# First halves of two experts filled from the scan's first three chunks, a reordered chunk, and rows kept by chunk

## Chip, core and metric

The program runs on one core of a Trainium2 chip. The metric is device time in microseconds (us) of one execution, the median of several. Five engines work beside each other, each through its own queue in order: TensorE (PE; its weight loads are shown apart as PEld), VectorE (DVE), ScalarE (ACT), GpSimd (POOL) and SyncE (SP). DMAs are issued from the queues of SP, ACT and POOL. An instruction that waits holds up everything behind it on its own engine.

## The reference

Two blocks follow each other. The first is a chunked state-space scan over 4 batches, 8 heads and 768 steps; the second sends each of the 3072 rows that come out (256 wide) to one of 8 experts, chosen by cosine similarity, and weighs the expert's output.

```python
# scan, per batch and head, chunk after chunk
cum = np.cumsum(la); L = np.exp(cum[:, None] - cum[None, :]) * causal
y[chunk] = ((C @ B.T) * L) @ x + (C @ state) * np.exp(cum)[:, None]
state = np.exp(sum(la)) * state + sum over j of exp(cum[-1] - cum[j]) * outer(B[j], x[j])
# rows: y laid out as (batch * step, head * dim), x below
logits = (x / norm(x)) @ (emb / norm(emb)).T / tau
e = argmax(logits); gate = softmax(logits)[e]
out = gate * (relu(x @ w1[e]) @ w2[e])          # w1: 256 x 1024, w2: 1024 x 256, float32
```

## The kernel before

**Scan.** `mamba` walks over six chunks of 128 steps (`NC` = 6), all four batches together. In chunk c TensorE spreads the decays of the next chunk, takes the inner products C B in two halves (`inner(k, c, 0)` and `inner(k, c, 1)`, into the four banks of `pg`), and VectorE masks each half (`mask_inner`, L336, 1536 elements wide). Between the two halves stands `finish(c-1)` (L395), which turns the previous chunk's outputs into rows and computes their logits; `keep_rows` copies the rows out of PSUM on ScalarE and `send_rows` stores them to `y_rows` in DRAM through SP. Then come the contributions of the states, the outputs of the two halves, `first_outputs`, and the state sums of the next chunk. GpSimd scales x of the next chunk (`scale_x`, `scale_first_half`) and makes U from T (`decay_states`); `add_sums` needs U at the next chunk's start.

**Routing beside the scan.** For each chunk, `pick` (VectorE) finds each token's expert and GpSimd adds the counts before every block of tokens into `pre`. `rank_rows` (two small matmuls) gives each token its rank in its expert, `places` (ten VectorE operations) turns ranks into a place: one of `NT` = 4 tiles of `TR` = 104 rows an expert, so 416 places. `locate` (eight matmul instructions, L580) writes the token's number to its place; the table `idx` is summed over chunks. At the end of each chunk stand, in this order: `pick(c-1)`, `decay_states(c+1)`, `places(c-2)`, `rank_rows(c-1)`, `locate(c-2)`. After the last chunk the remaining steps follow one after the other, and `end_places` makes the gather indices `gi` and the target rows `to`.

**Mixture.** A `Job` is one expert: four indirect gathers on GpSimd (L738) fetch its 416 rows; `turn_x` transposes them on TensorE; `gates` computes the weights, with squares and an exponential on ScalarE, a square root as a power on GpSimd (L759) and small VectorE steps; `up(f)` makes one of eight hidden blocks (L784; each float32 matmul shows as two instructions, so four a block), its result is copied through a ReLU by ScalarE and VectorE in turn; `down` makes the outputs (L798), `out` transposes them back (L812), multiplies by the gate (L814) and scatters the rows (L815). `moe` overlaps a job's `out` with the next job's `up`. Expert weights have three buffers. `leftover` is a loop for experts with more than 416 rows; where no expert has more, its blocks do not run.

The scan, up to `end_places`, is in an order written by hand (`manual_schedule`). The mixture is ordered by a scheduler, which also puts some of its instructions early: the weight loads of experts 1 and 2 were issued on SP between 42 and 69 us, ahead of later stores of rows.

Of the kernel before, what the change touches and what calls it, by code (L numbers as in the profile page):

```python
# [17 lines left out]
Q = 128  # L18
# [8 lines left out]
LEFT = (T - CAP) // Q + E  # L27
LG, Y1, W = 128, 128 + E, DM + E
# [379 lines left out]
def send_rows(k, c):  # L408
    k.nc.sync.dma_start(
        k.y_d.rearrange("(b c p) w -> c p b w", b=NB, p=Q)[c], k.ld[c].rows[:]  # L410
    )
# [50 lines left out]
def route_consts(k):  # L462
# [10 lines left out]
    k.tok1 = ints("tok1", [128, NC, NB], [[Q, NC], [S, NB]], 1, 1)  # L473
# [18 lines left out]
    k.idx = k.const.tile([TR, E * NT], F32, name="idx")  # L492
    k.at, k.eq, k.hot = {}, {}, {}
# [82 lines left out]
def locate(k, c):  # L576

    eq, hot = k.eq.pop(c), k.hot.pop(c)
    for b in range(NB):
        k.nc.tensor.matmul(  # L580
            k.pz[:TR, 1, 424 : 424 + E * NT], lhsT=hot[:, b, :],
            rhs=eq[:].rearrange("p (b e) t -> p b (e t)", b=NB)[:, b], start=(b == 0), stop=(b == NB - 1),
        )


def keep_located(k, c):
    if c == 0:
        k.nc.scalar.copy(out=k.idx[:], in_=k.pz[:TR, 1, 424 : 424 + E * NT])
        return
    i = k.work.tile([TR, E * NT], F32, name="ix", tag="ix")  # L590
    k.nc.scalar.copy(out=i[:], in_=k.pz[:TR, 1, 424 : 424 + E * NT])
    k.nc.gpsimd.tensor_tensor(out=k.idx[:], in0=k.idx[:], in1=i[:], op=ALU.add)


def end_places(k):
    nc = k.nc
    c = NC - 1
    locate(k, c)
    n = k.pz[:, 1, 456 : 456 + E]
    nc.tensor.matmul(n, lhsT=k.ones[:], rhs=k.pre[:, NU, :], start=True, stop=True)  # L600
    nc.vector.tensor_tensor(out=k.idx[:], in0=k.idx[:], in1=k.pz[:TR, 1, 424 : 424 + E * NT], op=ALU.add)
# [7 lines left out]
    nc.vector.scalar_tensor_tensor(  # L609
        out=k.to[:], in0=k.idx[:], scalar=-1.0, in1=none[:], op0=ALU.add, op1=ALU.add  # L610
    )
# [4 lines left out]
def mamba(k):  # L616
# [29 lines left out]
    for c in range(NC):  # L646
# [3 lines left out]
        if c in (3, 4):  # L650
            load_weights(k, 0, (c - 3,))
        if c + 1 < NC:
            spread_decays(k, c + 1)
# [3 lines left out]
        mask_inner(k, c, 0)  # L657
        if c + 1 < NC:
            scale_c(k, c + 1)
# [14 lines left out]
        if c + 1 < NC:  # L674
            split_b(k, c + 1)
            mask_c(k, c + 1)
            scale_x(k, c + 1, nc.gpsimd)
            scale_first_half(k, c + 1, nc.gpsimd)
            if c in (0, 3):
                between(k, c + 1, 4 if c == 0 else NC)  # L680
            pass_c(k, c + 1)
        if c == 0:
            decays(k, 1)
            block_ends(k, 1)
            inverses(k, 1)
# [3 lines left out]
        outputs(k, c, 1)  # L689
        first_outputs(k, c)  # L690
# [3 lines left out]
        if c == 1:  # L694
            turn_inverses(k, 1, k.pz[:, 0, 0:256])
        if c > 0:
            pick(k, c - 1)
        if c + 1 < NC:
            decay_states(k, c + 1)
        if c >= 2:  # L700
            places(k, c - 2)
        if c > 0:
            rank_rows(k, c - 1)
            keep_ranks(k, c - 1)
        if c >= 2:
            locate(k, c - 2)
            keep_located(k, c - 2)
    c = NC - 1
    finish(k, c)
    keep_rows(k, c)  # L710
    send_rows(k, c)
    places(k, c - 1)
    pick(k, c)
    locate(k, c - 1)
    keep_located(k, c - 1)
    rank_rows(k, c)
    keep_ranks(k, c)
    places(k, c)
    end_places(k)
    k.step = k.ints("step", [128, LEFT], [[1, LEFT]], 0, 0)  # L720
    k.part = k.ints("part", [128, 1], [[0, 1]], 0, 1)


class Job:


    def __init__(s, k, nt, tr, w1, w2):
        s.k, s.nt, s.tr, s.w1, s.w2 = k, nt, tr, w1, w2

    def load(s, e):  # L730
        k = s.k
        s.x = k.p.tile([s.tr, s.nt, KD * Y1], F32, name="xg", tag="xg")
        for i in range(s.nt):
            s.gather(i, k.gi[:, NT * e + i : NT * e + i + 1])
        s.to = k.to[:, NT * e : NT * e + NT]

    def gather(s, i, at):
        s.k.nc.gpsimd.indirect_dma_start(  # L738
            out=s.x[:, i, 0:W], out_offset=None, in_=s.k.y_d[:, :],
            in_offset=bass.IndirectOffsetOnAxis(ap=at, axis=0), bounds_check=T - 1, oob_is_err=False,  # L740
        )

    def gates(s):

        k, nc, tr, nt = s.k, s.k.nc, s.tr, s.nt
        m = k.p.tile([tr, nt], F32, name="gm", tag="gm")
        nc.vector.reduce_max(out=m[:], in_=s.x[:, :, LG : LG + E], axis=AX.X)  # L747
        l = k.p.tile([tr, nt, E], F32, name="gl", tag="gl")
        nc.vector.tensor_tensor(
            out=l[:], in0=s.x[:, :, LG : LG + E], in1=m[:].unsqueeze(2).to_broadcast([tr, nt, E]), op=ALU.subtract  # L750
        )
        r = k.p.tile([tr, nt], F32, name="gr", tag="gr")
        for i in range(nt):
            sq = k.p.tile([tr, KD, 128], F32, name="sq", tag="sq")
            nc.scalar.activation(  # L755
                sq[:], s.x[:, i, :].rearrange("p (j w) -> p j w", j=KD)[:, :, 0:128], ACT.Square,
                accum_out=r[:, i : i + 1],
            )
        nc.gpsimd.tensor_tensor(out=r[:], in0=r[:], in1=k.half[0:tr, 0:nt], op=ALU.pow)  # L759
        nc.vector.tensor_scalar_add(r[:], r[:], 1e-6)  # L760
        nc.vector.reciprocal(out=r[:], in_=r[:])
        nc.vector.tensor_tensor(out=l[:], in0=l[:], in1=r[:].unsqueeze(2).to_broadcast([tr, nt, E]), op=ALU.mult)
        nc.scalar.activation(l[:], l[:], ACT.Exp)
        s.gate = k.p.tile([tr, nt], F32, name="gate", tag="gate")
        nc.vector.reduce_sum(out=s.gate[:], in_=l[:], axis=AX.X)
        nc.vector.tensor_scalar_add(s.gate[:], s.gate[:], 1e-9)
        nc.vector.reciprocal(out=s.gate[:], in_=s.gate[:])

    def turn_x(s):
        k, nc, tr, nt = s.k, s.k.nc, s.tr, s.nt  # L770
        s.xT = k.p.tile([128, KD, nt * tr], F32, name="xT", tag="xT")
        for j in range(KD):
            t = k.ps.tile([128, nt, tr], F32, name="xt", tag="xt", bufs=2)
            for i in range(nt):
                nc.tensor.transpose(t[:, i, :], s.x[:, i, Y1 * j : Y1 * j + 128], k.ident[:tr, :tr])  # L775
            nc.vector.tensor_copy(out=s.xT[:, j, :], in_=t[:].rearrange("p t r -> p (t r)"))

    def up(s, f):
        k, nc = s.k, s.k.nc
        if f == 0:  # L780
            s.hT = k.p.tile([128, KF, s.nt * s.tr], F32, name="hT", tag="hT")
        t = k.ps.tile([128, s.nt * s.tr], F32, name="hp", tag="hp", bufs=3)
        for j in range(KD):
            nc.tensor.matmul(  # L784
                t[:], lhsT=s.w1[:, j, 128 * f : 128 * f + 128], rhs=s.xT[:, j, :], start=(j == 0), stop=(j == KD - 1)
            )
        if f % 2 == 0:
            nc.scalar.activation(s.hT[:, f, :], t[:], ACT.Relu)  # L788
        else:
            nc.vector.tensor_scalar_max(s.hT[:, f, :], t[:], 0.0)  # L790

    def down(s):
        k, nc = s.k, s.k.nc
        s.yT = k.p.tile([128, KD, s.nt * s.tr], F32, name="yoT", tag="yoT")
        for j in range(KD):
            t = k.ps.tile([128, s.nt * s.tr], F32, name="yp", tag="yp", bufs=2)
            for f in range(KF):
                nc.tensor.matmul(  # L798
                    t[:], lhsT=s.w2[:, f, 128 * j : 128 * j + 128], rhs=s.hT[:, f, :],
                    start=(f == 0), stop=(f == KF - 1),  # L800
                )
            if j % 2 == 0:
                nc.scalar.copy(out=s.yT[:, j, :], in_=t[:])
            else:
                nc.vector.tensor_copy(out=s.yT[:, j, :], in_=t[:])  # L805

    def out(s):
        k, nc, tr = s.k, s.k.nc, s.tr
        for i in range(s.nt):
            t = k.ps.tile([128, DM], F32, name="ot", tag="ot", bufs=1)  # L810
            for j in range(KD):
                nc.tensor.transpose(t[:tr, 128 * j : 128 * j + 128], s.yT[:, j, tr * i : tr * i + tr], k.ident[:])  # L812
            y = k.p.tile([tr, DM], F32, name="yo", tag="yo", bufs=4)
            nc.vector.tensor_scalar_mul(y[:], t[:tr, :], s.gate[:, i : i + 1])  # L814
# [9 lines left out]
def moe(k):  # L824
    jobs = {}

    def begin(e):
        jobs[e] = j = Job(k, NT, TR, k.w1t[e], k.w2t[e])
        j.load(e)

    def ready(e):
        jobs[e].turn_x()
        jobs[e].gates()

    begin(0)
    load_weights(k, 1)
    ready(0)
    load_weights(k, 2)
    begin(1)
    for e in range(E + 1):  # L840
        for f in range(KF):
            if e < E:
                jobs[e].up(f)
            if f == 1 and e > 0:
                jobs.pop(e - 1).out()
        if e + 1 < E:
            ready(e + 1)
        if e < E:
            jobs[e].down()
        if e == E // 2:  # L850
            leftover_blocks(k)
        if e + 2 < E:
            begin(e + 2)
        if e + 3 < E:
            load_weights(k, e + 3)
# [60 lines left out]
def leftover(k):  # L916
# [30 lines left out]
    with k.tc.For_i(0, blocks, 1) as i:  # L947
# [10 lines left out]
        j = Job(k, 1, Q, w1, w2)  # L958
# [20 lines left out]
        j.gather(0, to[:, 0:1])  # L979
        j.turn_x()  # L980
        j.gates()
        for f in range(KF):
            j.up(f)
        j.down()
# [4 lines left out]
def kernel(  # L989
# [22 lines left out]
    k.wp = ctx.enter_context(tc.tile_pool(name="wp", bufs=3))  # L1012
    with ExitStack() as m:
# [4 lines left out]
        k.pg = ps.tile([128, 4, 512], F32, name="pg")  # L1018
        k.py = ps.tile([128, 2, 512], F32, name="py")
        k.pz = ps.tile([128, 2, 512], F32, name="pz")  # L1020
# [52 lines left out]
```

## Time and profile before

| | us |
|---|---|
| median of 3 runs (lowest, highest) | 327.66 (327.49, 328.27) |
| profiled execution | 328.09 |
| its span, first to last instruction | 326.3 |
| TensorE busy | 274.3 |
| VectorE, ScalarE, GpSimd busy | 121.5, 65.0, 124.1 |
| mean granted TensorE clock, as a share of full speed | 0.913 |

The page's first part gives each engine's busy time; a busy engine is not always one that sets the end. The chain that ended last puts 58% of the span on TensorE, 17% on "issue" (time in which an engine waited for nothing that the profile shows), 11% on VectorE and 5% on GpSimd. Lines L798 and L784, the expert matmuls, make 41% of it.

In an engine's timeline each line has the start in us from the span's start, the duration in us, engine, line, operation, the tiles written and read, sizes, a count, and in brackets the idle time before it with what ended it.

### The profile page before, as it was taken

The numbers are of one execution on the slowest core, as the hardware profiler recorded it, in microseconds if no ns is written. First come the engines' busy times: TensorE is split into PE (matmuls) and PEld (weight loads), VectorE is DVE, ScalarE is ACT, GpSimd is POOL, SyncE is SP. The second block draws the span as 40 slices with busy tenths as digits, with TensorE's granted clock in tenths as the row PEclk, the third lists the DMA queues.
The fourth block names the chain that finished last, engine by engine and source line by source line (L and its number), as shares of the span: only waits on it lengthen the run. The fifth ranks groups of instructions, "written<-read, shape, count | busy, mean of one in ns | idle before, by whom it ended". The sixth has DMA issues, their size and how long they took to land.

```text
span 326.3 us, 5585 instructions
## 1 busy us (share of the span) xinstructions
PE 274.3 (84%) x2170; PEld 175.6 (54%) x2170; DVE 121.5 (37%) x337; ACT 65.0 (20%) x185; POOL 124.1 (38%) x174
## 2 busy tenths in 40 slices
PE   7878859768752868999999999999999999999700
PEld 6767749658641425555555555555555555555300
DVE  6486575772745323142142142142142042040210
ACT  3413413131311431210220210310310110111000
POOL 8975680440125853334344244254250040040130
PEclk9679996995985699999999999999999999999955
DMA  5975495995211223554454454355350010010010
GB/s 156 343 227 153 162 270 142 262 284 134 68 68 41 67 54 74 110 156 102 106 161 104 93 168 110 81 169 123 80 158 11 0 45 0 0 53 0 0 54 0
DMA packets 22299, 35.81 MB, mean 110 GB/s; under 512 B 2549, under 2 KB 15551, under 8 KB 22272
## 3 DMA queue, kind: packets, MB, share of 16 engines
q1 hardware_dynamic: 19024, 28.73, 31.8%
q0 software_dynamic: 3072, 6.67, 8.1%
q8 instruction: 17, 0.28, 0.4%
q14 instruction: 10, 0.08, 0.1%
q10 hardware_dynamic: 176, 0.06, 0.1%
HBM read 29.05 MB, written 6.65 MB: 109 GB/s over the span
## 4 chain that ended last, share of the span: by engine, by line
PE 58%; issue 17%; DVE 11%; POOL 5%; ACT 2%; DMA 2%; ACTq 0%; POOLq 0%; DVEq 0%
PE yp L798 21%; PE hp L784 20%; PE pg L326 5%; DVE g L336 4%; POOL out_dram L815 2%; PE pz L580 2%; PE ot L812 2%; POOL xg L738 2%; PE py L395 2%; PE pz L395 2%; PE xt L775 1%; PE py L377 1%; PE py L364 1%; POOL gr L759 1%; DMA xg<-y_rows,gi 1%
## 5 line engine op out<-in xcount | busy, mean ns | idle before, releaser
L784 PE MATMUL hp<-xT,w 128*128 128x416 f32 x256 | 98.0, 522 | 4.5 <-DVE hT L790 3.2
L798 PE MATMUL yp<-hT,w 128*128 128x416 f32 x256 | 90.8, 513 | 0.0
L798 PEld LDWEIGHTS yp<-hT,w 128*128 128x128 f32 x256 | 48.1, 190 | 38.5 <-issue 38.5
L784 PEld LDWEIGHTS hp<-xT,w 128*128 128x128 f32 x256 | 46.9, 193 | 38.4 <-issue 30.1
L815 POOL DMA_INDIRECT out_dram<-yo,to x32 | 32.4, 1012 | 86.9 <-DVE yo L814 80.2
L738 POOL DMA_INDIRECT xg<-y_rows,gi x32 | 35.0, 1095 | 33.6 <-PE xt L775 21.5
L790 DVE TENSOR_SCALAR hT<-hp 128x416 f32<-128x416 f32 x32 | 18.9, 590 | 45.4 <-PE hp L784 32.6
L788 ACT ACTIVATE hT<-hp 128x416 f32<-128x416 f32 x32 | 16.5, 516 | 74.1 <-PE hp L784 52.3
L336 DVE TENSOR_TENSOR g<-pg,mask 128x1536 f32<-128x1536 f32 x12 | 21.1, 1757 | 23.1 <-PE pg L326 23.1
L755 ACT ACTIVATE sq<-xg 104x256 f32<-104x256 f32 x32 | 13.2, 411 | 62.4 <-DMA xg<-y_rows,gi 62.4
L814 DVE TENSOR_SCALAR yo<-ot,gate 104x256 f32<-104x256 f32 x32 | 15.4, 480 | 11.8 <-PE ot L812 11.0
L747 DVE TENSOR_REDUCE gm<-xg 104x4 f32<-104x32 f32 x8 | 1.5, 186 | 45.5 <-DMA xg<-y_rows,gi 45.5
L805 DVE COPY yoT<-yp 128x416 f32<-128x416 f32 x8 | 4.7, 590 | 32.9 <-PE yp L798 22.2
L580 PE MATMUL pz<-eq,hot 128*104 128x32 f32 x48 | 7.2, 304 | 11.6 <-DVE hot L570 8.3
L759 POOL TENSOR_TENSOR gr<-gr,half 104x4 f32<-104x4 f32 x8 | 8.4, 1050 | 21.4 <-ACT sq L755 21.4
L812 PEld LDWEIGHTS ot<-ident,yoT 128*104 128x104 f32 x64 | 7.0, 132 | 16.6 <-DVE yo L814 8.5
L511 POOL TENSOR_TENSOR pre<-pre,ob 128x8 bf16<-128x8 bf16 x24 | 5.2, 218 | 28.0 <-DVE ob L509 17.7
L812 PE MATMUL ot<-ident,yoT 128*104 128x128 f32 x64 | 13.4, 290 | 2.4 <-DVE yo L814 1.7
L775 PE MATMUL xt<-ident,xg 104*128 104x104 f32 x64 | 8.6, 271 | 7.1 <-DMA xg<-y_rows,gi 7.1
L326 PE MATMUL pg<-cp,bi 32*128 32x128 f32 x192 | 13.4, 355 | 1.0 <-DVE cp L219 0.8
L580 PEld LDWEIGHTS pz<-eq,hot 128*104 128x104 f32 x48 | 6.6, 224 | 12.3 <-issue 8.5
L775 PEld LDWEIGHTS xt<-ident,xg 104*128 104x128 f32 x64 | 6.9, 148 | 10.7 <-issue 7.8
(172 smaller groups left out, 291.7 us busy)
## 6 DMA issues: line engine op xcount, KB each, us to landing
w<-in_moe_w_dram SPq DMA_DIRECT2D x16, 512.0 KB, 6.7
w<-in_moe_w_dram SPq DMA_DIRECT2D x8, 1024.0 KB, 11.7
y_rows<-rows SPq DMA_DIRECT2D x6, 528.0 KB, 4.2
x<-in_x_dram SPq DMA_DIRECT2D x6, 512.0 KB, 7.6
ct<-in_CT_dram SPq DMA_DIRECT2D x6, 256.0 KB
bi<-in_BT_dram SPq DMA_DIRECT2D x6, 256.0 KB, 5.3
b<-in_B_dram SPq DMA_DIRECT2D x6, 256.0 KB, 6.2
xa<-in_x_dram SPq DMA_DIRECT2D x6, 128.0 KB, 6.4
```

The costliest lines, as they stand in the source:

```text
L326: k.nc.tensor.matmul(k.pg[:, q, 192 * u + a : 192 * u + a + n], lhsT=m, rhs=x, start=True, stop=True, tile_position=(32 * q, 0),)
L336: k.nc.vector.tensor_tensor(out=g[:], in0=k.pg[:, :, 0:384].rearrange("p q (u m) -> p q u m", u=2), in1=k.mask[:].unsqueeze(1).unsqueeze(1 ...
L580: k.nc.tensor.matmul(k.pz[:TR, 1, 424 : 424 + E * NT], lhsT=hot[:, b, :], rhs=eq[:].rearrange("p (b e) t -> p b (e t)", b=NB)[:, b], start ...
L738: s.k.nc.gpsimd.indirect_dma_start(out=s.x[:, i, 0:W], out_offset=None, in_=s.k.y_d[:, :], in_offset=bass.IndirectOffsetOnAxis(ap=at, axis ...
L775: nc.tensor.transpose(t[:, i, :], s.x[:, i, Y1 * j : Y1 * j + 128], k.ident[:tr, :tr])
L784: nc.tensor.matmul(t[:], lhsT=s.w1[:, j, 128 * f : 128 * f + 128], rhs=s.xT[:, j, :], start=(j == 0), stop=(j == KD - 1))
L788: nc.scalar.activation(s.hT[:, f, :], t[:], ACT.Relu)
L790: nc.vector.tensor_scalar_max(s.hT[:, f, :], t[:], 0.0)
L798: nc.tensor.matmul(t[:], lhsT=s.w2[:, f, 128 * j : 128 * j + 128], rhs=s.hT[:, f, :], start=(f == 0), stop=(f == KF - 1),)
L812: nc.tensor.transpose(t[:tr, 128 * j : 128 * j + 128], s.yT[:, j, tr * i : tr * i + tr], k.ident[:])
L814: nc.vector.tensor_scalar_mul(y[:], t[:tr, :], s.gate[:, i : i + 1])
L815: d = nc.gpsimd.indirect_dma_start(out=k.out[:, :], out_offset=bass.IndirectOffsetOnAxis(ap=s.to[:, i : i + 1], axis=0), in_=y[:], in_offs ...
```

## The change

- The rows in `y_rows` are ordered by chunk, then batch, then step, so chunks 0 to 2 are the first 1536 rows. `tok1` numbers tokens so; `out_rows` computes the target row in the output from such a number.
- Within a chunk: `rank_rows(c-2)` and `locate(c-3)` now stand between the two inner products, ahead of `finish(c-1)`; at the end stand `places(c-2)`, `decay_states(c+1)`, `pick(c-1)`. The addition to `idx` on GpSimd stands behind the scaling of x.
- After chunk 2 is counted, `shift_places` raises the counts of experts 0 and 1 to 208 (half of their places) where they are lower, so what comes later lands in the second half. In chunk 5 `early_places` makes indices from chunks 0 to 2 and gathers two tiles each for experts 0 and 1.
- Experts 0 and 1 are each worked on as two jobs of two tiles (208 columns). The two first halves (`first`, `second`) run in the hand-written order in `scan_end`, between the steps of the turn; their results go to the four banks of `pg` in rotation and are copied by ScalarE alone, except for half of the down results. The second halves (`late`) are gathered after `end_places` and are worked on at the head of the mixture; then come experts 2 to 7 as before.
- `gates` becomes `all_gates`, taken once for the two first halves together and once for the two second halves.
- Weights of expert 1 are loaded at chunk 5 (w1) and after chunk 5's rows (w2), those of expert 2 after that.

The diff, cut to its core:

```diff
 def send_rows(k, c):
-        k.y_d.rearrange("(b c p) w -> c p b w", b=NB, p=Q)[c], k.ld[c].rows[:]
+        k.y_d.rearrange("(c b p) w -> c p b w", b=NB, p=Q)[c], k.ld[c].rows[:]
...
+        if c == 5:
+            load_weights(k, 1, (0,))
...
         inner(k, c, 0)
         mask_inner(k, c, 0)
+        if c >= 2:
+            rank_rows(k, c - 2)
+            keep_ranks(k, c - 2)
+        if 3 <= c < NC - 1:
+            locate(k, c - 3)
+            keep_located(k, c - 3)
+        if c == NC - 1:
+            early_places(k, c - 3)
...
+        if 3 <= c < NC - 1:
+            add_located(k, c - 3)
...
         outputs(k, c, 1)
+        if c == NC - 1:
+            early = early_jobs(k)
+            early[0].turn_x()
         first_outputs(k, c)
         keep_outputs(k, c)
...
+        if c >= 2:
+            places(k, c - 2)
+        if c == 4:
+            shift_places(k)
+        if c + 1 < NC:
+            decay_states(k, c + 1)
         if c > 0:
             pick(k, c - 1)
-        if c + 1 < NC:
-            decay_states(k, c + 1)
-        if c >= 2:
-            places(k, c - 2)
-        if c > 0:
-            rank_rows(k, c - 1)
-            keep_ranks(k, c - 1)
-        if c >= 2:
-            locate(k, c - 2)
-            keep_located(k, c - 2)
...
+def scan_end(k, early):
+    first, second = early
+    first.up(0)
+    rank_rows(k, c - 1)
+    keep_ranks(k, c - 1)
+    first.up(1)
     finish(k, c)
     keep_rows(k, c)
     send_rows(k, c)
+    load_weights(k, 1, (1,))
+    second.w2 = k.w2t[1]
     places(k, c - 1)
     pick(k, c)
+    first.up(2)
+    first.up(3)
+    locate(k, c - 2, 0, True, False)
+    locate(k, c - 1, 0, False, False)
+    first.up(4)
     rank_rows(k, c)
     keep_ranks(k, c)
     places(k, c)
+    for f in (5, 6, 7):
+        first.up(f)
+    second.turn_x()
+    first.down(0)
+    locate(k, c, 0, False, True)
     end_places(k)
+    late = late_jobs(k)
+    load_weights(k, 2)
+    first.down(1)
+    gates = all_gates(k.ep, k, k.early_x, TR, NT)
...
+    second.up(0)
+    second.up(1)
+    first.out()
+    for f in range(2, KF):
+        second.up(f)
+    late[0].turn_x()
+    gates = all_gates(k.ep, k, k.late_x, TR, NT)
...
+    second.down(0)
+    second.down(1)
...
+def early_places(k, c):
+    locate(k, c)
+    nc.vector.tensor_tensor(out=k.idx[:], in0=k.idx[:], in1=ps, op=ALU.add)
+    nc.vector.tensor_scalar(out=gi[:], in0=k.idx[:], scalar1=-1.0, scalar2=0.0, op0=ALU.add, op1=ALU.max)
+    k.early_x = gather_halves(k, gi, 0, 3 * NB * Q)
...
+def gather_halves(k, gi, t, rows=T):
+    for e in range(2):
+        for i in range(HT):
+            gather(k, x[:, HT * e + i, 0:W], gi[:, NT * e + t + i : NT * e + t + i + 1], rows)
...
+def shift_places(k):
+    nc.tensor.matmul(n, lhsT=k.ones[:], rhs=k.pre[:, NB * 3, :], start=True, stop=True)
+    nc.vector.tensor_scalar(out=t[:], in0=n, scalar1=-1.0, scalar2=float(HALF), op0=ALU.mult, op1=ALU.add)
+    nc.vector.scalar_tensor_tensor(
+        out=t[:], in0=t[:], scalar=0.0, in1=k.shifted[:], op0=ALU.max, op1=ALU.mult
+    )
+    nc.vector.tensor_tensor(out=p, in0=p, in1=t[:], op=ALU.add)
...
+def late_jobs(k):
+    x = k.late_x = gather_halves(k, k.gi, HT)
...
+        if f % 2 == 0 or s.bank_ is not None:
+            nc.scalar.activation(s.hT[:, f, :], t, ACT.Relu)
...
+def moe(k, second, late):
+    jobs = list(late)
+    for j in jobs:
+        j.bank_ = None
+    last = second
+    e = 2
+    jobs.append(begin(e))
+    while i < len(jobs) or last is not None:
+        for f in range(KF):
+            if j is not None:
+                j.up(f)
+            if f == 1 and last is not None:
+                last.out()
+        if i + 1 < len(jobs):
+            ready(jobs[i + 1])
+        if j is not None:
+            j.down(0)
+            j.down(1)
+        if i >= 0 and e + 1 < E and i != 0:
+            e += 1
+            jobs.append(begin(e))
+        if i == 0:
+            load_weights(k, 3)
+        elif i >= 1 and e + 1 < E:
+            load_weights(k, e + 1)
```

`next_bank` hands out the four banks of `pg` in turn. `out_rows` is five VectorE operations where `end_places` had one.

## The prediction

> **What bounds the kernel now.** The slices come first: they split the span into a scan (to about 83 us), a turn into the mixture (to about 127 us) and seven even periods.
>
> ```profile
> ## 2 busy tenths in 40 slices
> PE   7878859768752868999999999999999999999700
> PEclk9679996995985699999999999999999999999955
> ```
>
> From the 17th slice on (8.16 us each) TensorE is full at full clock; before that it has holes and the granted clock falls with them. TensorE's timeline gives the holes and the fixed pieces:
>
> ```profile
> 47.24 1.38 PE L580 MATMUL pz<-eq,hot 128*104 128x32 f32 x8 [3.75 <-DVE hot L570]
> ...
> 72.99 0.92 PE L377 MATMUL py<-g,xb 128*64 128x64 f32 x23 [2.34 <-issue]
> ...
> 103.74 0.58 PE L775 MATMUL xt<-ident,xg 104*128 104x104 f32 x2 [5.10 <-DMA xg<-y_rows,gi]
> ...
> 108.66 7.65 PE L784 MATMUL hp<-xT,w 128*128 128x416 f32 x16 [0.51 <-DVE xT L776]
> ```
> ```profile
> 126.48 0.88 PE L775 MATMUL xt<-ident,xg 104*128 104x104 f32 x8
> 127.20 11.36 PE L798 MATMUL yp<-hT,w 128*128 128x416 f32 x32
> ...
> 295.46 11.34 PE L798 MATMUL yp<-hT,w 128*128 128x416 f32 x32
> ```
>
> The reader is to see three things. From 127.20 to 306.64 TensorE never waits: one job is 32 instructions up (11.17 us at 0.349), 32 down (11.2), 8 transposes in (0.72), outputs (1.2), a period of 24.14. From the last down to the span's end another 19.66 us pass. And between 83.31, where the scan's last mask starts, and 127.20, TensorE does only 11.2 us of expert work in 43.9 us. VectorE's timeline shows what paces the scan:
>
> ```profile
> 38.91 1.76 DVE L336 TENSOR_TENSOR g<-pg,mask 128x1536 f32<-128x1536 f32 x1 [1.24 <-PE pg L326]
> ...
> 43.53 1.99 DVE L561 TENSOR_TENSOR eq<-rk,first_of 128x128 f32<-128x128 f32 x1
> 45.55 1.04 DVE L565 TENSOR_TENSOR eq<-eq,tok 128x128 f32<-128x128 f32 x1
> ...
> 55.78 1.76 DVE L336 TENSOR_TENSOR g<-pg,mask 128x1536 f32<-128x1536 f32 x1 [2.39 <-PE pg L326]
> ```
>
> Second masks of chunks 2 to 5 start at 38.91, 55.78, 67.74 (from the chain) and 83.31: intervals of 16.87, 11.96 and 15.57. In the first, two operations that take 0.29 each in a later chunk take 3.0 together while GpSimd scales x (43.41 to 48); the third holds the 2.34 us issue gap. In both the granted clock averages 0.80 and 0.78, against 1.00 in the middle one.
>
> **Part 1, the reordered scan.** `places(c-2)` now stands before T, and U and the scaling of x on GpSimd start after T, so the collision of the first interval goes. In exchange `rank_rows(c-2)` stands in mid-chunk and waits for the pick and GpSimd's `pre` adds; queued behind it on TensorE are `locate`, `finish` and the second inner product. The new cycle from second mask to second mask: mask 1.76, places 2.38 (85.97 to 88.35), T 0.34, pick 1.06, three of four pre adds with hand-off 0.95, rank with its copy 0.5 (93.86 to 94.36), locate 0.89, its copy 0.33, finish 2.12 (63.76 to 65.88), inner 1.09: 11.4. In chunk 5 `shift_places` adds three small operations, 0.55. So 11.4 + 11.4 + 12.0 = 34.8 against 44.4: -9.6. What this takes for granted is that the issue gap goes too; its cause is not in the rows, so I leave 1.7 of it (2.34 with some slow clock, at half weight): **-7.9**. Bounds: 0, all holes return elsewhere; -9.6. On SP, expert 1's w1 (1 MB) moves to chunk 5, its w2 behind chunk 5's rows, expert 2's behind that; before, all of these were issued between 42 and 69 us, where the DMA share was 0.83 to 1.01. They are needed 20 us or more after the new issue and take 6.7 to 11.7: nothing. Stores keep their 528 KB. The last mask starts at 83.3 - 7.9 = 75.4.
>
> **Part 2, half jobs beside the turn**, in us after that mask's start. A half job streams 208 columns: 0.349 / 2 = 0.175 an instruction, 0.70 per hidden block, 5.6 up, 5.6 down, 0.35 transposes. Four halves cost TensorE what two whole jobs did. Early gathers need only chunks 0 to 2. They are issued behind `locate(2)`, beside `finish(4)` and the second inner product (3.2 us), 2 to 3 us before the mask; the second lands 4.6 us after the first's start (100.18 to 104.77), at +1.8 to +2.8, and TensorE reaches `turn_x` at +2.5. If they are later, `first_outputs` and `finish(5)` behind it slip one for one. Then:
> - mask, outputs, turn, first outputs, up 0: +4.7. Rank of chunk 4 waits for places 2.38, pick 1.06, pre 0.95 after the mask: +6.2, a 1.5 us hole.
> - rank 0.3, up 1 0.7, finish 2.1, up 2 and 3 1.4 (covering the row copies, 1.1), two locates 1.8, up 4 0.7, rank 0.2, up 5 to 7 2.1, turn 0.35, down 2.8, locate 0.9, counts 0.2: +19.75. Each piece was a wait before; now expert work fills it.
> - down 2.8, up 0 and 1 of the second half job 1.4, output transposes 0.6: +24.55.
> - The new wait: `all_gates`' square root on GpSimd stands behind four late gathers. Indices at +20.4 (0.73 from counts to gi), 1.0 to the first gather, 5.5 for four (100.18 to 105.64), root 1.05, and 1.25 to the end of Exp (122.64 to 123.89): +29.2. ScalarE holds Exp at its queue's head, and behind it the copies of up 0 and 1 (about 0.35, estimated from 0.516 for twice the columns): +29.6. TensorE has four banks, so up 2 stands 5.0 us. The profile of before has the same chain: a root at 121.59, and first-job ups taking 17.8 us for 11.17 of work.
> - up 2 to 7 4.2, turn 0.35, down 5.6: +39.75. After the 3.75 us hole at 47.24 eight locates took 1.38 instead of 0.89 and the slow stretch lasted to 54.6. For 5 us of standing I add 2.75, between 0 and 3.7 (half of 7.4): **+42.5**.
>
> The five operations of `out_rows` replace one; VectorE then waits for the root, which hides them (0.8 without that cover). The late gathers land some 5 us before their transposes.
>
> The Trainium skill, "TensorE: Matmul & The Clock Gate", section "What's actually happening", has the array back at full rate after about 3.4 us of busy time; by that the loss would be 1.7 and the total 1 us lower. The trace's stretch of 7.4 us is longer, and I go by it.
>
> **Part 3, the rest.** Two late halves: 5.6 + 0.6 + 0.35 + 5.6 = 12.1, and 12.5 with a whole turn. Expert 2: 11.17 + 0.6 + 0.72 + 11.2 = 23.7; four at 24.14; the last 23.4. Sum 168.3. Weight reloads wait for late halves now, yet have over 30 us. Leftover blocks would cost a loop; evaluating the reference's routing gives experts 0 and 1 202 and 165 tokens in chunks 0 to 2, 206 and 183 after. Filled to 208, they need 414 and 391 places of 416: none.
>
> **The sum.** 75.4 + 42.5 + 168.3 + 19.66 = 305.9 of span, against 326.3. The profiled execution took 328.09, 1.8 more than its span, and stands 0.43 above the median: 305.9 + 1.8 - 0.4 = **307.3 us**.
>
> **Rivals.**
> *The scan gives nothing* (0.2): the rank's wait in mid-chunk takes the place of the one at the end. For it: 11.4 is hardly under the undisturbed 11.96. Against it: the two other intervals hold 8.5 us above that. Price 7.9: 315.
> *The turn runs better* (0.2): scheduler or data place the root ahead of the gathers. Without the 5.0 hole and the 2.75 of clock: 299.5. Against it: GpSimd's order here is written by hand.
> *Root later still* (0.1): expert 2's four gathers slip in front of it, as expert 1's did before the first root here (105.94 to 111.2). Price 5.5: 313.
> *Weight loads bound the half-width matmuls* (0.06), the slower side. It decides from (327.7 - 307.3) / 256 = 0.08 us above 0.175 for each of the four halves' 256 instructions. For it: the profile's mean load at the expert lines is 190 to 193 ns, which by itself, not hidden behind 175, would add 3.8 us; load and stream in series, 0.365, would add 49: 356. Against it, chunk rows:
>
> ```profile
> 64.33 1.09 PE L395 MATMUL py<-turn,yT 128*128 128x136 f32 x8
> 65.25 0.63 PE L395 MATMUL pz<-turn,yT 128*128 128x136 f32 x4
> ```
>
> Eight matmuls with a 128x128 load each start within 0.92 us, 0.115 apiece, so the load hides under even 136 columns.
>
> The Trainium skill speaks against halving in the same page, "Why this matters for your kernels": with under 512 moving rows the clock oscillates unless contractions stay contiguous. At half clock the four halves would cost 44.8 more; the row above, at full clock with 136 columns, disagrees.
>
> **How the numbers follow.** Forecast 0.44, own range 302 to 312; the rivals 0.2, 0.2, 0.1, 0.06. The range of 8 in 10 takes the full scan gain with the better turn (298) up to no scan gain with a longer hole (318). A measurement here tells 0.3% (1 us) from no change. Slower holds the weight-load case and 0.02, taken from the forecast's, for an unseen stall of over 20 us: 0.08; the same another 0.02; faster 0.90.
>
> **What would show it.** Second masks 11 to 12.5 us apart; early transposes before the last `finish` without a DMA wait over 1 us; half-width matmuls 0.175 apart; one hole of 4 to 6 us at the second half job's third block, ended by ScalarE, whose Exp follows the root; whole jobs still 24.14; last down near 286. Half-width spacing of 0.19 or more, a hole before the early transposes, or loops on the leftover lines would prove it wrong.

## The result and the profile after

The changed kernel takes 343.48 us (median of 4 runs, 339.41 to 347.71), the kernel before, on the same chip, 327.97 (4 runs, 327.49 to 328.32): slower by a ratio of 1.039 (95% interval 1.032 to 1.047), where 307.3 us and a gain were forecast. Each ratio in this document compares only those runs of a kernel that lie within 1.5% of its fastest, which here leaves out two of the changed kernel's four, the profiled one among them. The profiled execution took 344.85 us with a span of 343.0. Its last down ends at 323.7, where the forecast's steps put it at 286.2: 37.5 us are to be found.

The slices of the changed kernel (8.58 us each) show where. Up to the 12th TensorE is about as busy as before, and its clock dips less; from the 13th to the 18th (103 to 154 us), where the second half job and the first late one run, TensorE has its emptiest slices, and in four of the six its clock is near half.

```profile
## 2 busy tenths in 40 slices
PE   6968988968875778469988999999999999999800
...
PEclk9669999889998555859998999999999999999965
```

VectorE's timeline of the changed kernel has the second masks of chunks 2 to 5:

```profile
40.99 1.76 DVE L337 TENSOR_TENSOR g<-pg,mask 128x1536 f32<-128x1536 f32 x1 [1.52 <-PE pg L327]
...
52.56 1.76 DVE L337 TENSOR_TENSOR g<-pg,mask 128x1536 f32<-128x1536 f32 x1 [3.09 <-PE pg L327]
...
65.82 1.76 DVE L337 TENSOR_TENSOR g<-pg,mask 128x1536 f32<-128x1536 f32 x1 [4.37 <-PE pg L327]
...
80.66 1.76 DVE L337 TENSOR_TENSOR g<-pg,mask 128x1536 f32<-128x1536 f32 x1 [6.12 <-PE pg L327]
```

The scan did become shorter, but by 2.7 us (83.31 to 80.66) and not by 7.9. TensorE's timeline of the half jobs and what follows them:

```profile
94.22 0.97 PE L899 MATMUL pg<-xT,w 128*128 128x208 f32 x4 [0.33 <-ACT hT L903]
95.63 0.97 PE L899 MATMUL pg<-xT,w 128*128 128x208 f32 x4 [0.43 <-ACT hT L903]
97.03 0.97 PE L899 MATMUL pg<-xT,w 128*128 128x208 f32 x4 [0.43 <-ACT hT L903]
...
111.69 1.76 PE L899 MATMUL pg<-xT,w 128*128 128x208 f32 x4 [3.90 <-ACT hT L903]
...
118.62 1.75 PE L899 MATMUL pg<-xT,w 128*128 128x208 f32 x4 [0.43 <-ACT hT L903]
120.80 1.75 PE L899 MATMUL pg<-xT,w 128*128 128x208 f32 x4 [0.43 <-ACT hT L903]
...
131.10 5.74 PE L913 MATMUL pg<-hT,w 128*128 128x208 f32 x16 [0.60 <-ACT xT L889]
...
148.65 0.67 PE L926 MATMUL pg<-ident,yoT 128*104 128x128 f32 x2 [7.34 <-DVE yo L928]
...
162.96 1.57 PE L899 MATMUL hp<-xT,w 128*128 128x208 f32 x8
...
181.56 0.46 PE L926 MATMUL ot<-ident,yoT 128*104 128x128 f32 x1 [3.10 <-DVE yoT L919]
```

Three things are to be seen. Blocks of the half jobs start 1.40 us apart where 0.70 was forecast: each waits for ScalarE's copy (`hT`) of the block before, although that block lies in another of the four banks of `pg`. The hole that ends at 111.69 was forecast, a block later; behind it they start 2.19 apart, and a half-width down of 16 instructions takes 5.74 where its fellow at full clock (137.26) takes 3.08. And behind the second half job stands a hole of 7.34, with a smaller one at expert 2, neither of them forecast. Late halves, by contrast, run their blocks without a wait, at 0.175 us an instruction at full clock: 8 in 1.41 us from 162.96 to 164.37. The windows put numbers to the clock (after the busy times come the granted clock, the DMA share and GB/s):

```profile
84.00:106.80 22.80, 18.75 (x142) 16.38 (x136) 8.61 (x40) 8.04 (x25) 3.77 (x10) 1.00 0.65 167
106.80:140.40 33.60, 24.36 (x72) 17.97 (x72) 7.32 (x36) 6.66 (x23) 10.83 (x14) 0.59 0.09 24
```

### The profile page after: what moved, and what is told of

It is laid out like the page before. It is cut to its first block, busy times and chain, and to the rows that moved or that the text cites. A ratio compares the mean times of both kernels' runs of the same rounds, so it can differ in the third digit from the quotient of the medians.

```text
span 343.0 us, 5864 instructions
## 1 busy us (share of the span) xinstructions
PE 286.7 (84%) x2299; PEld 202.3 (59%) x2299; DVE 118.6 (35%) x345; ACT 71.2 (21%) x203; POOL 123.3 (36%) x173
## 4 chain that ended last, share of the span: by engine, by line
PE 55%; issue 19%; DVE 9%; POOL 9%; ACT 3%; DMA 1%; SPq 0%; POOLq 0%; DVEq 0%; ACTq 0%
PE hp L899 17%; PE yp L913 15%; PE pg L899 5%; PE pg L327 4%; POOL xg L797 4%; DVE g L337 3%; POOL out_dram L929 2%; PE pz L396 2%; PE py L396 2%; PE ot L926 1%; PE pz L584 1%; ACT hT L903 1%; POOL gr L958 1%; DMA x<-in_x_dram 1%; PE xt L886 1%
## 5 line engine op out<-in xcount | busy, mean ns | idle before, releaser
L899 PE MATMUL hp<-xT,w 128*128 128x416 f32 (+1 forms) x256 | 87.0, 485 | 0.0
L913 PE MATMUL yp<-hT,w 128*128 128x416 f32 (+1 forms) x256 | 79.8, 470 | 0.0
L905 DVE TENSOR_SCALAR hT<-hp 128x416 f32<-128x416 f32 (+1 forms) x32 | 17.2, 536 | 41.6 <-PE hp L899 31.6
L903 ACT ACTIVATE hT<-hp 128x416 f32<-128x416 f32 (+1 forms) x32 | 15.2, 474 | 73.6 <-PE hp L899 58.1
L899 PE MATMUL pg<-xT,w 128*128 128x208 f32 x64 | 20.9, 463 | 8.8 <-ACT hT L903 7.7
L899 PEld LDWEIGHTS pg<-xT,w 128*128 128x128 f32 x64 | 14.1, 248 | 14.7 <-ACT hT L903 12.7
L928 DVE TENSOR_SCALAR yo<-ot,gate 104x256 f32<-104x256 f32 x28 | 13.4, 480 | 11.9 <-PE ot L926 11.9
L919 DVE COPY yoT<-yp 128x416 f32<-128x416 f32 (+1 forms) x8 | 4.3, 537 | 37.7 <-PE yp L913 27.0
L913 PE MATMUL pg<-hT,w 128*128 128x208 f32 x64 | 15.0, 397 | 1.6 <-ACT xT L889 1.2
L913 PEld LDWEIGHTS pg<-hT,w 128*128 128x128 f32 x64 | 13.5, 226 | 2.7 <-ACT xT L889 1.7
L946 DVE TENSOR_REDUCE gm<-xg 104x4 f32<-104x32 f32 x8 | 1.5, 183 | 33.0 <-DMA xg<-y_rows,gi 32.8
L959 DVE TENSOR_SCALAR gr<-gr 104x4 f32<-104x4 f32 x8 | 1.4, 170 | 32.8 <-POOL gr L958 32.8
```

The source lines that it names most:

```text
L899: nc.tensor.matmul(t, lhsT=s.w1[:, j, 128 * f : 128 * f + 128], rhs=s.xT[:, j, :], start=(j == 0), stop=(j == KD - 1))
L903: nc.scalar.activation(s.hT[:, f, :], t, ACT.Relu)
L905: nc.vector.tensor_scalar_max(s.hT[:, f, :], t, 0.0)
L913: nc.tensor.matmul(t, lhsT=s.w2[:, f, 128 * j : 128 * j + 128], rhs=s.hT[:, f, :], start=(f == 0), stop=(f == KF - 1))
L928: nc.vector.tensor_scalar_mul(y[:], t[:tr, 0:DM], s.gate[:, i : i + 1])
```

## The experiments

Runs of one kernel differ here by up to 4%, and in the 13 traces with the changed kernel's scan the last second mask starts anywhere from 77.5 to 89.7 us. So beside each time stands a stretch of its profiled execution that leaves the scan out: from the start of the last second mask to the start of the last job's down. It is 212.2 us before (83.31 to 295.46) and 231.7 after (80.66 to 312.36); the forecast's steps make it 199.5 (42.5 + 168.3 - 11.3).

**Four banks as four tiles (e1_banks).** The pool of `pg` is closed after chunk 5's second mask has read it, and the half jobs rotate through four tiles of a bank each.

```diff
+            k.banks = [eb.tile([128, 512], F32, name=f"eb{i}") for i in range(4)]
...
-            return k.pg[:, k.bank_no % 4, :]
+            return k.banks[k.bank_no % 4]
```

> Four one-bank tiles take the place of the one four-bank tile pg for the half jobs, all else as in the changed kernel. Theory A (a copy from one bank of a shared tile holds up the matmuls into the next bank): blocks of a half job follow each other 0.70 to 0.75 us apart instead of 1.41 and 2.19, second half job's ups and downs at full clock, time 322 to 330 us. Theory B (only the hole before the second half job's blocks counts, because it drops the clock): the hole stays 4 to 5 us, blocks after it at half clock, time 336 to 342. Theory C (the scheduler's order behind the second half job is the main loss): 338 to 342, with the wait of 7 us before the late jobs kept.

324.9 us median (5 runs, 322.43 to 333.02); ratio to the kernel before 0.989 (0.980 to 0.998). Time and spacing are as theory A had them. The stretch is 211.0, 20.7 less than after; the profiled execution itself was the longest of the five, as its last second mask starts 9 us later than the changed kernel's (89.65). TensorE's timeline of this kernel:

```profile
102.06 2.36 PE L900 MATMUL eb<-xT,w 128*128 128x208 f32 x12
...
116.61 4.49 PE L900 MATMUL eb<-xT,w 128*128 128x208 f32 x24 [3.56 <-ACT hT L904]
120.93 0.52 PE L887 MATMUL eb<-ident,xg 104*128 104x104 f32 x4
121.29 5.81 PE L914 MATMUL eb<-hT,w 128*128 128x208 f32 x32
...
138.90 7.42 PE L900 MATMUL hp<-xT,w 128*128 128x208 f32 x20 [6.90 <-ACT hT L904]
```

Three blocks in 2.2 us, 0.73 each, and the whole second half job's down in 5.65. The hole of the root is still there (3.56), but behind it the clock is 1.00 (116.6 to 121 us). So the waits come from the four banks being one tile, and where they stand the half job runs at a slower clock too: from the last second mask to the end of the second half job pass 37.3 us (89.65 to 126.94) in place of 59.7 (80.66 to 140.34). What stays is a hole behind it, now 6.90.

**The second half job's outputs in written order (e2_out).** The changed kernel, with `second.out()` at the end of `scan_end`.

```diff
     second.down(1)
+    second.out()
```

> The second half job's output is put into the hand-written order, behind its down; all else as in the changed kernel. Theory C: the 7.3 us wait of TensorE between the two output transposes goes to about 1 us: 334 to 338 us. Theory A: 5 to 8 us less as well, since this wait stands beside the shared tile, but the spacing of 1.41 and 2.19 us of the blocks stays. If that wait was covered anyway: 342 to 345.

343.75 (4 runs, 340.86 to 347.24), ratio 1.042 (1.028 to 1.055); stretch 230.7. The 7.34 went, and holes of 2.30, 2.05 and 3.06 opened inside the first late job. Nothing is gained by this alone. This trace, of 342.5 us, repeats the changed kernel's: blocks 1.40 apart, a hole of 3.90, then blocks 2.19 apart.

**The root moved behind the second half job's blocks (e3_root).** The changed kernel, with the early gates and the first outputs after all eight blocks.

```diff
+    for f in range(KF):
+        second.up(f)
     gates = all_gates(k.ep, k, k.early_x, TR, NT)
-    second.up(0)
-    second.up(1)
     first.out()
-    for f in range(2, KF):
-        second.up(f)
```

> The early gates (square root on GpSimd, exponential on ScalarE) and the first half job's output stand behind the second half job's eight blocks; the shared tile stays. Theory A alone: the hole of 4 us before the second block goes, blocks stay 1.4 us apart at full clock: 336 to 340 us. Theory B (the hole drops the clock and the gaps between blocks keep it low): no hole, blocks 1.41 instead of 2.19 apart, downs 2.9 instead of 5.74 each: 324 to 331.

339.46 (4 runs, 336.94 to 339.79), ratio 1.029 (1.019 to 1.038); stretch 227.8. Its TensorE timeline:

```profile
111.21 0.97 PE L897 MATMUL pg<-xT,w 128*128 128x208 f32 x4 [0.43 <-ACT hT L901]
112.62 0.97 PE L897 MATMUL pg<-xT,w 128*128 128x208 f32 x4 [0.43 <-ACT hT L901]
...
122.13 0.67 PE L924 MATMUL pg<-ident,yoT 128*104 128x128 f32 x2 [4.87 <-DVE yo L926]
```

The same 0.43 waits now leave the clock at 1.00 (100 to 116 us) and the blocks 1.40 apart. It took the hole to halve it. But the root's time comes back as a hole of 4.87 in front of the outputs.

**The scan alone (e4_scan, e5_weights).** The mixture of before, with the reordered chunk and the rows by chunk; in the second kernel all weight loads of experts 0 to 2 stand after chunk 5's rows.

```diff
-        if c in (3, 4):
-            load_weights(k, 0, (c - 3,))
...
+    for e in range(3):
+        load_weights(k, e)
```

> The kernel before with the chunk's steps reordered and rows kept by chunk, but with no early half jobs: eight whole jobs as before. By the prediction's first term 318 to 322 us. If the reordered scan only moves its waits: 326 to 329. By the changed kernel's trace (last mask at 80.7 against 83.3): 323 to 327.

> The reordered scan with eight whole jobs, all weight loads of experts 0 to 2 moved out of the scan, behind the last rows. Theory F (TensorE's issue gaps in the scan are waits of its instruction loads behind bulk loads): no issue gap over 0.5 us after 45 us, chunks 11.4 to 12 us apart at full clock, last second mask near 74 to 77 us instead of 86 to 88, time 316 to 322 us. If the gaps have another cause: gaps stay, 327 to 333. If the loads, now later, delay the first job: its first blocks wait for a DMA, up to 8 us given back.

The first takes 332.04 (10 runs, 322.66 to 334.16): above all three ranges named for it, with nine of the ten runs at 329.9 or more. In its profiled execution the second masks of chunks 2 to 5 stand at 39.54, 52.74, 66.88 and 86.13, the last interval with this wait on TensorE:

```profile
74.31 1.55 PE L378 MATMUL py<-g,xb 128*64 128x64 f32 x24 [4.59 <-issue]
```

The DMA share is 1.07 to 1.10 in the 4.8 us before it, and 1.06 to 1.11 beside two further such gaps of 1.49 and 1.85. With the loads moved no issue gap over 0.5 us is left in those chunks; the masks stand at 38.66, 51.85, 63.47 and 76.30: 37.6 us for three intervals, 6.8 less than the 44.4 of before. That is nearly the forecast's 7.9. But the time, expected at 316 to 322, is 330.92 (12 runs, 327.53 to 339.75), ratio 1.008 (1.001 to 1.015): the loads now run beside the first job's gathers,

```profile
106.02 1.16 PE L806 MATMUL xt<-ident,xg 104*128 104x104 f32 x4 [10.95 <-DMA xg<-y_rows,gi]
```

with a DMA share of 1.06 to 1.07 and a clock of 0.50 from 90 to 110 us. That the issue gaps go with the bulk loads rests on more than this one trace, but is not proved. With three experts' loads issued between 42 and 72 us (before, e4_scan, e8_beforehand) each trace has issue gaps over 1 us after 45 us; with one and a half (the changed kernel's scan) two of 13 traces have, and e5_weights, with none, has not. What TensorE waits for is told by the DMA packets: the gap of 4.59 begins at 69.72, and a 16 KB packet of the DMA queue that the profile names `instruction` (q8) runs from 71.42 to 72.77, 1.54 us before TensorE goes on. In all 17 traces each of the 31 issue gaps over 0.6 us ends 1.2 to 1.6 us after such a packet has ended. So these gaps are waits for instructions, as theory F had it; that the packet comes late because of the bulk loads is argued from the counts above.

**The whole mixture in written order (e6_hand, e7_root, e8_beforehand).** The four tiles, the outputs of the second half job in `scan_end`, and all of `moe` under `manual_schedule`; the same with the root moved; and, as a control, the kernel before with its mixture so.

```diff
-        moe(k, early[1], late)
+        with tc.manual_schedule():
+            moe(k, early[1], late)
```

> One-bank tiles, and the whole mixture in the written order (the second half job's output at the end of the turn) instead of the scheduler's. Theory C (after the shared tile, what is left is the scheduler putting gates that wait for gathers ahead of the late jobs' copies): the holes of 2.1, 6.9 and 3.5 us behind the second half job go, 308 to 315 us. If those holes only move, as they did when the output alone was put by hand: 321 to 327.

> As the run before, and the early gates and the first half job's output behind the second half job's blocks. By the prediction's term of the root: the hole of 3.6 us before the third block goes, 304 to 311 us, 3 to 5 us under the run before. If the gates are then late for the output: no gain, or 1 to 2 us more.

> The kernel before with only its mixture in the written order. Theory C for the changed kernel says that the order matters where jobs are short; here, with jobs of 24 us, 326 to 330 us: the first job's blocks may gain up to 3 us, since expert 1's gathers no longer stand ahead of the first root.

All three lie above what was expected: 328.24 (10 runs, 327.5 to 330.61), ratio 1.000 (0.996 to 1.004), stretch 217.2; 333.96 (4 runs, 327.43 to 336.51), stretch 220.8; and the control 353.38 (4 runs, 347.08 to 357.94), ratio 1.061 (1.051 to 1.071). The holes behind the second half job go, yet from one whole job's down to the next pass 26 to 33 us in place of 24.14: in written order the pairs of output transposes wait 0.58 to 0.86 each (4.36 once) for VectorE to clear the one bank that they share. The control has the same waits (26.6 to 32.1 a job), so this is a cost of the written order and not of the change. The scheduler spreads those transposes between blocks.

**Expert 2's gathers earlier (e9_free, e10_both, e11_freeonly).** In the changed kernel the gathers of expert 2 are issued from 135.67 on, right behind two number tables of GpSimd's (134.18) whose end frees the scan's memory. Here the tables stand behind the early gates, with the four tiles; with the root moved too; and with the shared tile.

```diff
+    k.step = k.ints("step", [128, LEFT], [[1, LEFT]], 0, 0)
+    k.part = k.ints("part", [128, 1], [[0, 1]], 0, 1)
     second.up(0)
...
-    k.step = k.ints("step", [128, LEFT], [[1, LEFT]], 0, 0)
-    k.part = k.ints("part", [128, 1], [[0, 1]], 0, 1)
```

> The four one-bank tiles, and GpSimd's step and part numbers moved up to right behind the early gates, so that the scan's memory is released earlier and expert 2's gathers can be issued earlier. Theory C (what is left behind the second half job is that expert 2's gathers are issued only at 135.67, behind the step and part numbers at 134.18, while its gates already stand ahead of the late jobs' copies): the gathers are issued over 15 us earlier, the holes of 6.90 before the second half job's copies and of 3.52 before expert 2 go, and the time is 310 to 316, against the four banks alone at 322 to 325. Rival (the holes only move, as they did with the outputs by hand): 322 to 326.

> As the former, and the early gates and the first outputs behind all eight blocks of the second half job. Theory C and the root's hole together: no hole at the second half job's third block (3.6 us with the four banks) and no slow clock behind it, 306 to 312. If the hole only moves to the second half job's down, as it did with the shared tile, no less than the former kernel.

> The changed kernel with its shared tile, and the step and part numbers moved up alone. Theory C says that the late gathers are a cost of their own beside the shared tile: 331 to 337 against the changed kernel's 343.5. Rival (blocks 1.40 apart leave time enough, or the holes move): 341 to 345.

323.99 (4 runs, 321.53 to 328.36), 327.16 (324.91 to 329.97) and 341.13 (339.02 to 342.36), beside a kernel before of 330.75 (7 runs, 323.83 to 332.6); stretches 210.7, 212.9 and 230.1, against 211.0 with the tiles alone and 231.7. The gathers do come earlier (from 105.63), and nothing is gained: theory C falls. ScalarE's timeline of e9_free shows why, and TensorE's shows the price:

```profile
110.14 0.42 ACT L955 ACTIVATE sq<-xg 104x256 f32<-104x256 f32 x1 [0.68 <-DMA xg<-y_rows,gi]
...
111.52 0.42 ACT L955 ACTIVATE sq<-xg 104x256 f32<-104x256 f32 x1 [0.87 <-DMA xg<-y_rows,gi]
...
111.94 0.33 ACT L904 ACTIVATE hT<-eb 128x208 f32<-128x208 f32 x1
```
```profile
121.98 5.95 PE L914 MATMUL eb<-hT,w 128*128 128x208 f32 x18 [3.45 <-ACT hT L904]
```

The scheduler has set the squares of the next experts' gates between the copies (`hT`) of the second half job. Each square waits for its own gather, and the copy behind it waits with it. From the root's hole at 105.37 to the end of the second half job pass 22.4 us, for 10.2 us of work at full clock.

**The transition in written order (e12_late, e13_next, e14_gates, e15_gates3).** e9_free, with the second half job's outputs in `scan_end`, and `manual_schedule` kept up for the first two jobs of `moe`, the late ones; for one job more; the former with the early gates ahead of the late gathers; and both.

```diff
+    hand = ExitStack()
+    hand.enter_context(k.tc.manual_schedule())
...
+        if i == 2:
+            hand.close()
```
```diff
     places(k, c)
+    gates = all_gates(k.ep, k, k.early_x, TR, NT)
     for f in (5, 6, 7):
         first.up(f)
```

> The four one-bank tiles, the step and part numbers early, and the second half job's outputs, both late jobs and expert 2's gates in written order, the rest as before. In the kernel without the written order ScalarE's squares of expert 2's gates stood between the second half job's copies, each behind a gather, and its six last blocks and its down took 22.5 us for 10.2 of work. Theory D (what is left of the forecast's gain lies in where the gates of the next jobs are put): no such wait, the stretch from the last second mask to the start of the last down is 199 to 205 us in place of 210.7, and the time 311 to 318. Rival (the holes move again, as in every order so far): a stretch of 209 to 217, 321 to 328.

> As the former (stretch of 207.8 us from the last second mask to the start of the last down, 317.9 us), with the written order kept up for one job more, through expert 2. Theory D: the hole of 6.27 at 153.27 (VectorE's copy of the late job's outputs behind the gates of experts 3 and 4, which the scheduler had put ahead of it) goes; a stretch of 200 to 204 and 310 to 315 us. Rival (the same hole opens one job later, or the outputs in written order cost as much): 206 to 210, 316 to 320.

> As the first kernel with the written order (207.8, 317.9 us), with the early jobs' gates, their square root on GpSimd among them, set ahead of the late gathers instead of behind them. If the root behind four gathers is the cause of the 3.55 us hole at the second half job's third block: no hole there, a stretch of 203 to 205 and 313 to 316. Rival (the gates delay the ranks of chunk 5, and the late gathers with them): no change or a loss, 207 to 211.

> Both edits together: the forecast's own case with neither of its waits. If both causes are what they are taken for, they add: a stretch of 196 to 201 and 306 to 312 us. If they share a cause or the holes move, no better than the better of the two alone.

| | median us (runs, lowest to highest) | ratio to before | stretch |
|---|---|---|---|
| e12_late | 317.93 (6, 316.26 to 323.14) | 0.967 (0.961 to 0.972) | 207.8 |
| e13_next | 317.48 (4, 316.61 to 318.29) | 0.968 (0.960 to 0.975) | 206.0 |
| e14_gates | 318.58 (4, 316.62 to 321.32) | 0.971 (0.961 to 0.981) | 207.1 |
| e15_gates3 | 317.23 (5, 316.72 to 320.98) | 0.966 (0.959 to 0.974) | 205.8 |

All four beat both kernels; among themselves their intervals don't tell them apart. TensorE's timeline of e13_next:

```profile
105.16 6.04 PE L901 MATMUL eb<-xT,w 128*128 128x208 f32 x24 [3.54 <-ACT hT L905]
111.03 0.52 PE L888 MATMUL eb<-ident,xg 104*128 104x104 f32 x4
111.39 5.81 PE L915 MATMUL eb<-hT,w 128*128 128x208 f32 x32
...
118.04 5.79 PE L901 MATMUL hp<-xT,w 128*128 128x208 f32 x32
...
156.36 11.36 PE L915 MATMUL yp<-hT,w 128*128 128x416 f32 x32
...
176.66 0.45 PE L928 MATMUL ot<-ident,yoT 128*104 128x128 f32 x1 [4.72 <-DVE yoT L921]
```

From the last second mask (78.24) to the end of the second half job (117.04) pass 38.8 us, and to the end of expert 2's down (167.55) 89.3. The forecast's own steps say 42.5 and 90.8 (42.5 + 12.1 + 12.5 + 23.7). The rest of the stretch is the hole at 176.66 and a slow clock behind it, one job later than in e12_late, where it was 6.27 at 153.27: it sits each time at the first job that the scheduler orders. The early gates (e14_gates) take the root's hole away, and waits of 2.38, 1.57 and 1.14 come instead. So theory D holds for the transition, though e12_late's stretch of 207.8 lies between its 199 to 205 and the rival's 209 to 217. Neither of the last two edits paid, and both together are no better than either: e13_next, e14_gates and e15_gates3 came out as was expected for the case that the holes move.

## Why the prediction was wrong, point by point

- **The step that failed** is in part 2: "TensorE has four banks", from which blocks 0.70 us apart followed for both half jobs. The banks are parts of one tile, and its matmuls waited for the copy out of another bank, 0.43 us a block. With the clock this made 59.7 us of part 2's 42.5: 17.2 of the 37.5. Giving each bank a tile of its own took 22.4 off part 2 and 20.7 off the stretch, more than the 19.5 that the changed kernel's stretch lost to the one before. The trace of before had spoken against the assumption, in a TensorE row of which the prediction makes nothing:

```profile
89.72 0.73 PE L395 MATMUL pz<-turn,yT 128*128 128x136 f32 x4 [0.33 <-ACT ix L591]
```

  `finish` writes one bank of the two-bank tile `pz` here and waits for ScalarE's read of the other. The Trainium skill, "Perfetto Trace Analysis", section "Optimizing Tensor Performance", advises rotating independent groups of matmuls through different PSUM banks, so that copies out run beside the next group. The runs agree where each bank is a tile (0.73 a block) and not where four banks are one tile (1.40).
- **The second failed step** is part 3's price of the late jobs and expert 2, taken as if nothing stood in front of them. The scheduler orders that part and set the next experts' gates ahead of the outgoing job's copies: 7.34 and 3.10 of hole in the changed kernel, with some slow clock. VectorE's timeline of the changed kernel has the 7.34: the copy `yo` of the outgoing job stands behind a reduction (L946) that waits for expert 2's gathers and a step (L959) that waits for GpSimd's root, which stands behind eight gathers.

```profile
143.12 0.18 DVE L946 TENSOR_REDUCE gm<-xg 104x4 f32<-104x32 f32 x1 [2.29 <-DMA xg<-y_rows,gi]
147.74 0.17 DVE L959 TENSOR_SCALAR gr<-gr 104x4 f32<-104x4 f32 x1 [4.44 <-POOL gr L958]
147.82 0.38 DVE L1054 TENSOR_REDUCE left_n<-mine_not 128x28 f32<-128x224 f32 x1
148.12 0.48 DVE L928 TENSOR_SCALAR yo<-pg,gate 104x256 f32<-104x256 f32 x1
```

  From the end of the second half job to the end of the last down it took 183.4 (140.34 to 323.7) where 168.3 were forecast: 15.1 more. The profile of before had the pattern too: the prediction cites the first job's ups, 17.8 us for 11.17 of work, but for the root alone. In written order through expert 2 the late jobs and expert 2 took 50.5 (117.04 to 167.55) for 48.3.
- **The scan** was mis-sized: 80.66 in place of 75.4, the last 5.3. The cycle itself was right at full clock (11.6 for 11.4, from 40.99 to 52.56), but the first of the four masks stands 2.1 us later than before (in traces with this scan it lies anywhere from 38.2 to 42.7), and in the two later intervals (13.3, 14.8) the clock fell to 0.87 and 0.89. Each fall is one stretch of half clock of 3.4 us (61.4 to 64.9 and 75.1 to 78.5), worth 1.7 us of work; the forecast left 1.7 in all, for an issue gap with some slow clock. Without issue gaps the three intervals were worth 6.8. What starts a fall is open: in e5_weights the clock fell to 0.87 in two intervals as well, with hardly any DMA beside one of them, so the loads aren't all of it.
- **The root's hole** was right in cause: ScalarE's copy behind the Exp, 3.90 where 5.0 was written; with the four tiles it stands at the second half job's third block, as written, and with the shared one at its second. The 2.75 of slow clock behind it was far too little with the shared tile. With four tiles and nothing else in the way (e1_banks, e13_next, e12_late, e6_hand) the six blocks took 4.3 to 7.35 in place of 4.2, a loss of 0.1 to 3.15.
- **The rival of the weight loads** fell: half-width matmuls are 0.175 apart at full clock. Whole jobs kept 24.14 (from 192.38 to 216.52, expert 2's down to expert 3's). The early transposes had no wait for their gathers.
- **The range** left out what decided: 0.02 was given to an unseen stall of over 20 us, and it was a wait at every block, two holes of 7.34 and 3.10, and a clock that lengthened both.

So the change's idea is sound and its making costs it: 317.2 to 318.6 us with the tiles apart and a written transition, about half of the forecast's gain, against 307.3 forecast. In e13_next's profiled execution (316.74 us) the difference is 9.4: 6.5 in the stretch (206.0 for 199.5), 2.8 in the scan (78.24 for 75.4).

## What to carry to other kernels

When a plan rests on several PSUM banks in rotation, look in the trace for one instruction that writes one bank while another engine reads the next; a wait there says that the banks are one thing to the program, and the plan's rhythm may double, as it did here. When work is overlapped by moving the start of a queue forward, ask what the scheduler will let slip in between: an operation that waits for a gather, put ahead of a copy on the same engine, stops TensorE two engines away. And after a hole, price the clock with the rhythm that follows it, not by itself.

## What the hardware showed that was not expected

The clock went with the hole and the gaps behind it together. With blocks 1.40 us apart and 0.43 idle in each, it stayed at 1.00 (e3_root, 100 to 116 us). After a hole of 3.90 the same blocks ran at half clock from 111.69 to the down at 131.10, at a mean of 0.59 from 106.8 to 140.4. After holes of 3.54 to 3.56 with no gaps behind them, six blocks took 4.3 us in e1_banks, 5.9 in e13_next, 7.2 in e12_late and 7.35 in e6_hand, in place of 4.2, and the down ran at full clock in all four. Why equal holes cost so differently can be seen in the clock records kept with the traces: up to the last entry of each, every stretch at one clock is a whole number of steps of 3.41 us. Behind these holes no step was slow in e1_banks, one in e13_next and two in e12_late and e6_hand; in the changed kernel it was eight.

The Trainium skill, "TensorE: Matmul & The Clock Gate", section "Why this matters for your kernels", warns of idle gaps over about 3 us. The changed kernel's 3.90 agrees; but e1_banks kept 1.00 through 3.56, and in the changed kernel's scan the clock was 0.50 from 62 to 64 us with no gap over 0.84 in the 30 us before. The same page's section "What's actually happening" has full rate back after a busy window of some 3.4 us. e13_next agrees (0.52 from 105.16 to 108.5, 1.00 behind it), and the changed kernel does not: with 0.43 us of idle in each 2.19 the clock stayed at 0.50 from 111.7 to 131.1. In e2_out, with the same hole and gaps, it was back at 127.4, before the last gap (129.2). That the gaps keep it down is therefore likely, but not shown.

TensorE's issue gaps do not all stand beside a high DMA share: it is 1.09 over the 4.59 us of e4_scan and 1.07 over the 2.34 of the kernel before, but 0.36 over a gap of 3.12 in e1_banks (58.02 to 61.14), and at 48 to 50 us of the changed kernel it is 1.08 without a gap. What they have in common is the packet of instructions that ends 1.2 to 1.6 us before they do.
